# Column-tiled matmuls of a four-layer attention kernel: two tiles of 64 columns instead of four of 32, and a matmul of 33 columns that gives a unit's numerator and denominator

## The chip, the cores and the metric

The kernel runs on one core of one Trainium2 chip. The metric is the device time of one execution in microseconds (us), lower is better. TensorE is called PE here, VectorE DVE, ScalarE ACT, GpSimd POOL and SyncE SP, as in the profile.

## The reference, cut to what matters

Four residual layers follow each other on x (2048 rows of 1024, bf16): A, B, A, B. Each normalizes the rows, projects to q, k and v in 32 heads of 32 columns, mixes, and projects back. A is a linear attention, with a feature map made of two softmaxes. B is softmax attention:

```python
scores = jnp.einsum("bhqd,bhkd->bhqk", q, k) * (Dh ** -0.5)
p = _softmax(scores, axis=-1)
o = jnp.einsum("bhqk,bhkd->bhqd", p, v)
return (lambda x, *d: x.transpose(*d))(o, 0, 2, 1, 3).reshape(B, S, D) @ wo

x = x + _A_ref(_layernorm(x, axis=-1), A_wqkv, A_w_phi, A_wo)
x = x + _B_ref(_layernorm(x, axis=-1), B_wqkv, B_wo)
x = x + _A_ref(_layernorm(x, axis=-1), A_wqkv, A_w_phi, A_wo)
x = x + _B_ref(_layernorm(x, axis=-1), B_wqkv, B_wo)
```

## The kernel before, in words

The program is a list of operations (engine, duration, what it waits for, buffers, priority) and a planner, `Sched.run`, that lays them out when the kernel is built. The planner keeps a clock of its own for each engine, takes the ready operation of the lowest priority number whose buffers can be had, and so writes a fixed order of instructions for each engine. On the chip an engine works through its own order and waits on semaphores. Durations and latencies (`LAT`, `act_us`, `dve_us`, `MM`, `SWITCH`) only shape this order, and some sixty constants (`KL`, `P0`, `MOST`, `LOAD` and the like) set due times and limits. A pair of an A and a B layer is one turn of `for layer in range(2)`: layer 0 and layer 1 below mean these pairs.

**Attention.** The queries are four chunks of 512 (`qc`), the heads eight groups of four (`g`). A turn is one (qc, g): 2 x 8 x 4 = 64 units, each 128 keys by 512 queries of one head, so 32 turns and 2048 units in each layer. For a unit the kernel makes scores on PE (L1191; a contraction of 32, so up to four units stand on different row tiles of the array and run together), the exponential, and the product with V (L1386). The functions:

- `group` takes up to three units from the front, has PE write their scores into one half (three banks) of six PSUM banks, and ACT takes the exponential of all of them in one instruction (L1251, 1536 wide). The two halves alternate.
- With a "third", it takes only two units for ACT (1024 wide), and the third bank goes to a unit some 25 ahead, which DVE makes into an exponential. It does so only if at least `MIX` groups lie between, if DVE's queue is below `THIRD_LOAD`, and if bank 7 is taken. `attach` adds a fourth unit in bank 7 where that is free and DVE's queue allows (`BOTH_LOAD`, `LOAD`). `MOST` limits the DVE units of a turn; it is 0 in the first turn of each layer.
- DVE's exponential is a conversion out of PSUM (`convert`, L1339) for each unit, and then for a batch of `NB` = 2 units `exp_dve`: two masks (L1153) and two tensor_tensor (L1158).
- The product with V: for two units four matmuls of 32 columns each, tile positions 0, 32, 64 and 96: V of one head and a block of ones, for each unit. So numerators stand in 64 rows of the accumulator bank 6, and the denominators, 32 times over, in the other 64; for the other pair of heads (`pp` = 1) the halves change places. `T` is the copy out of PSUM (L1402). Denominators go through 2 KB transfers (L1436), a reciprocal (L1441), a scratch tensor and a broadcast back (L1442, L1444), one transfer (L1447) brings the second pair's numerators beside the first's, and L1449 multiplies.

**Fillers between.** While attention runs, PE also computes the projections that are due (`mmg2`, which calls `mm`; with bank list `FIL`, that is bank 7 alone, `mm` splits each matmul into four of 32 columns at L584, so that the array stays in column tiling), in layer 0 also the keys of the next A layer (`a_keys` with `alone`, L836). Where the plan finds PE's last 3.4 us less than 75% worked it puts in matmuls of no use (`idle` through L584 with `onesD`, `idle_acc` at L1644 with zero weights). Outside attention, matmuls use the whole array (L580).

A change between row tiles, column tiles and the whole array is a "mode" of the planner ("r", "c", "n"), with `SWITCH` = 0.106 us for each change.

**V.** `b_v` projects V for 128 keys and 512 columns and evacuates it (`evac`, L1053 on ACT or L1054 on DVE) with the columns of each head side by side. **Output.** `b_out` multiplies the `oT` tiles with `B_wo`, loaded by `slab` in four transfers of 256 KB. The last turn of a layer (`end`) has a path of its own without transfers.

Of the kernel before, what the change touches and what calls it, by code (L numbers as in the profile page):

```python
# [11 lines left out]
ALU = mybir.AluOpType  # L12
# [12 lines left out]
class Buf:  # L25


    __slots__ = ("kind", "size", "cls", "banks", "left", "at", "with_", "key")

    def __init__(self, kind, size, cls, banks=None):  # L30
        self.kind, self.size, self.cls, self.banks = kind, size, cls, banks
        self.left, self.at, self.with_ = 0, None, ()

# [12 lines left out]
LAT = {"PE": 0.28, "ACT": 0.07, "DVE": 0.17, "POOL": 0.2, "SP": 2.0, "AQ": 2.0}  # L46
# [13 lines left out]
class Sched:  # L60
    def __init__(self, sbuf_bytes, quota):
# [7 lines left out]
        self.queue = {}  # L69
        self.idle = self.idle_acc = self.wants = self.pace = None  # L70
# [124 lines left out]
    def run(self):  # L195
# [28 lines left out]
        while left:  # L224
            moved = False
            for e in engines:
                if busy[e] > t + 1e-9 or not ready[e] and (e != "PE" or t < WARM_UP):
                    continue
                skipped, held = [], []
# [88 lines left out]
                busy[e] = t + d  # L318
                order.append(pick)
# [56 lines left out]
XQ = 7.72  # L376
# [9 lines left out]
NB = 2  # L386
SPLIT = (lambda i: False, lambda i: False)
LAG = 8
KL = (17, 32)
KS = (3.31, 6.5)  # L390
VS = (5, 6.75)
# [7 lines left out]
KD = 9.84  # L399
HALF = (False, True)  # L400
VH = 3.5
V_LATE = (None, ((8.47, 5.81), (77.66, 6.67)))
Q_LATE = (lambda c, g: 105 + 6 * g if c == 2 else 10.43 + 22.43 * g, lambda c, g: 120 + 12 * g)
QL = (11, 11.19)
AW = 26
OUT_AT = (232, 260.02, 273.59)
GO = 2.54
BO = 290.14
PT = 3.13
QB = 18.16  # L410
PH = (1, 22, 43)
LA = 1.59
AHEAD_AT = 4
P0 = (131.15, 178.4, 234.98)
GAPS = (1.5, 1.5, 3.19)
PK = (142, 184, 261.5)
STEP = 2.4
AWAY = (-10, 12)
MIX = (lambda i: (2, 2, 1, 2)[i // 8], lambda i: (0, 0, 0, 0)[i // 8])
LOAD = (2.03, 2.38)  # L420
AHEAD = (24, 25)
SLACK = 12
THIRD_LOAD = (3.79, 1.29)
BOTH_LOAD = (0.74, 0.56)
EARLY = (80, 80)
BEHIND = -4
NEAR = (8, 8)
LEAD = 0.14
MOST = (lambda i: 0 if i < 1 else 15, lambda i: 0 if i < 1 else 26)
# [10 lines left out]
MM = 0.2165  # L440
WARM = 60
WIRE = 360.0
BACKLOG = 1.0
KV_MM = 0.042
# [3 lines left out]
def kernel(  # L448
# [26 lines left out]
    B_o = B_wo.rearrange("(po pi) f -> pi po f", pi=P)  # L475
# [13 lines left out]
    zero = const.tile([P, DH], BF16, tag="zero")  # L489
# [19 lines left out]
    work = const.tile([P, 2, NB * C512], BF16, tag="work")  # L509
# [51 lines left out]
    def fixed(cls, spots):  # L561
        b = Buf("ps", 0, cls, spots)
        return b, lambda: work[:, b.at[0] - 8, :].rearrange("p (a b) -> p a b", b=C512)

# [12 lines left out]
    def mm(out_, lhsT, rhs, start, stop, cols):  # L577
# [4 lines left out]
        for k in range(4):  # L582
            ks = slice(32 * k, 32 * k + 32)
            nc.tensor.matmul(out_[ks, :], lhsT=lhsT[:, ks], rhs=rhs, start=start, stop=stop,  # L584
                             tile_position=(0, 32 * k), skip_group_check=True)

    MM4 = 0.2165
# [577 lines left out]
    def attention(base, kT, vT, q_of, gate, most, mix, turns, pos, ahead, near, load, split_at, early, third_load, both_load):  # L1165
# [166 lines left out]
        def convert(so, u, s_b, s_v, turn):  # L1332
# [10 lines left out]
            if k == NB - 1:  # L1343
                close(pair)
# [335 lines left out]
```

## Time and profile before

| what | us |
|---|---|
| median of 3 runs (2149.93 to 2153.79) | 2151.93 |
| the profiled execution | 2151.16 |
| its span, first to last instruction | 2149.0 |
| stretch 0 to 324, layer 0's linear attention and projections | 324 |
| stretch 324 to 1176, layer 0's softmax attention | 852 |
| stretch 1176 to 1376, layer 1's linear attention and projections | 200 |
| stretch 1376 to 2136, layer 1's softmax attention | 760 |

In the views, "busy" of an engine is the union of its instructions' times; a matmul is shown some 0.38 us long although the next starts 0.22 us later, since matmuls are pipelined, and an ACT or DVE instruction also overlaps the next a little. So a mean duration is longer than the step from one start to the next, and steps are read from the timeline. In a line of the grouped views stand line, engine, operation, output and input, shapes, count, then busy us and the mean ns of one, then idle time before them. "128*32" is a matmul on 128 rows and 32 columns of the array.

### The profile page before, as it was taken

How to read it: one execution, taken by the hardware profiler on the slowest of the kernel's cores; microseconds unless marked ns; L12 is line 12 of the kernel's file. 1: busy time of each engine (PE TensorE's matmuls, PEld its weight loads, DVE VectorE, ACT ScalarE, POOL GpSimd, SP SyncE). 2: the span in 40 equal slices, each digit the busy share in tenths (PEclk: the TensorE clock that was granted, in tenths of full speed). 3: DMA queues.
4: the chain of work that ended last, by engine and by line, in shares of the span. 5: the costliest groups of instructions: out<-in, count | busy, mean ns of one | idle time of the engine just before them, and what ended most of it. 6: DMA issues, size and time to landing. Idle time of an engine off the chain costs nothing. (4 is left out here: it accounts for less than half of the span.)

```text
span 2149.0 us, 64468 instructions
## 1 busy us (share of the span) xinstructions
PE 2104.6 (98%) x27498; PEld 784.6 (37%) x27498; DVE 1742.8 (81%) x3163; ACT 1934.9 (90%) x2050; POOL 27.4 (1%) x78
## 2 busy tenths in 40 slices
PE   9999999999999999999999999999999999999999
PEld 5543443333333333333333434533333333333333
DVE  8866552666567889997887876289999999999998
ACT  7337669999999999999999576899999999999998
POOL 1000000000000000000000000000000000000000
PEclk9999999999999999999999999999999999999999
DMA  7730231112233433342454312211111222121111
GB/s 232 162 71 14 75 78 26 33 45 54 59 94 94 120 101 110 93 139 58 128 156 138 110 40 69 62 30 35 39 47 43 52 52 55 38 71 54 49 44 36
DMA packets 258392, 161.53 MB, mean 75 GB/s; under 512 B 150712, under 2 KB 232632, under 8 KB 258104
## 3 DMA queue, kind: packets, MB, share of 16 engines
q1 hardware_dynamic: 258104, 157.41, 27.4%
q8 instruction: 215, 3.52, 0.7%
q14 instruction: 73, 0.60, 0.1%
HBM read 90.51 MB, written 29.87 MB: 56 GB/s over the span
## 5 line engine op out<-in xcount | busy, mean ns | idle before, releaser
L1251 ACT ACTIVATE arena<-psum 128x1536 bf16<-128x1536 f32 (+1 forms) x1349 | 1578.4, 1370 | 6.7 <-PE psum L1191 5.1
L584 PE MATMUL psum<-arena 128*32 128x512 bf16 (+1 forms) x9536 | 632.3, 365 | 7.0 <-DVE arena L814 1.7
L1386 PE MATMUL psum<-arena 128*32 128x512 bf16 x4096 | 608.2, 383 | 4.1 <-DVE arena L1402 3.0
L1386 PE MATMUL psum<-arena,ones_bf 128*32 128x512 bf16 x4096 | 608.0, 383 | 0.5 <-issue 0.5
L1191 PE MATMUL psum<-arena 32*128 32x512 bf16 x4096 | 530.7, 384 | 18.4 <-ACT arena L1251 15.5
L1339 DVE TENSOR_SCALAR arena<-psum 128x512 uint16<-128x512 f32 x618 | 417.8, 682 | 91.6 <-PE psum L1191 86.2
L580 PE MATMUL psum<-arena 128*128 128x512 bf16 (+1 forms) x1968 | 435.1, 372 | 2.2 <-DVE arena L848 0.7
L1158 DVE TENSOR_TENSOR arena<-arena,work 128x1024 bf16<-128x1024 bf16 x618 | 424.1, 686 | 13.3
L1191 PEld LDWEIGHTS <-arena 32*128 32x128 bf16 x4096 | 146.7, 91 | 553.3 <-issue 549.6
L584 PEld LDWEIGHTS <-arena 128*32 128x32 bf16 x9536 | 210.5, 95 | 257.2 <-issue 158.1
L580 PEld LDWEIGHTS <-arena 128*128 128x128 bf16 x1968 | 185.7, 98 | 217.7 <-issue 19.4
L1386 PEld LDWEIGHTS <-arena 128*32 128x32 bf16 x4096 | 165.3, 95 | 212.7 <-issue 150.1
L1153 DVE TENSOR_SCALAR work<-arena 128x1024 uint16<-128x1024 uint16 x618 | 239.3, 417 | 2.4
L1386 PEld LDWEIGHTS <-ones_bf 128*32 128x32 bf16 x4096 | 163.8, 95 | 25.1 <-issue 9.0
L1054 DVE CAST arena<-psum 128x512 bf16<-128x512 f32 (+1 forms) x120 | 69.3, 577 | 60.8 <-PE psum L584 47.5
L801 ACT ACTIVATE arena<-psum 128x512 bf16<-128x512 f32 x80 | 43.5, 594 | 71.7 <-PE psum L580 57.4
L1402 DVE COPY arena<-psum 128x512 f32<-128x512 f32 x126 | 85.8, 681 | 12.4 <-PE psum L1386 11.6
L805 DVE TENSOR_REDUCE arena<-arena 128x32 f32<-128x1024 bf16 x64 | 77.6, 1213 | 16.2 <-ACT arena L801 15.9
L953 ACT ACTIVATE arena<-psum 128x512 bf16<-128x512 f32 x112 | 61.9, 597 | 31.6 <-PE psum L580 28.7
L626 ACT ACTIVATE arena<-xR 128x1024 bf16<-128x1024 bf16 x40 | 42.3, 1057 | 44.9 <-DVE xR L1028 39.0
L814 DVE TENSOR_TENSOR arena<-psum,arena 128x1024 bf16<-128x1024 f32 x64 | 77.6, 1212 | 4.0 <-DVE arena L808 0.4
L1028 DVE TENSOR_TENSOR xR<-xR,psum 128x512 bf16<-128x512 bf16 x64 | 42.6, 682 | 15.1 <-PE psum L580 15.0
(98 smaller groups left out, 1008.4 us busy)
## 6 DMA issues: line engine op xcount, KB each, us to landing
arena<-in_B_wqkv_dram SPq DMA_DIRECT2D x69, 256.0 KB
arena<-rd SPq DMA_DIRECT2D x62, 256.0 KB
xa<-arena SPq DMA_DIRECT2D x48, 256.0 KB
arena<-in_A_wqkv_dram SPq DMA_DIRECT2D x40, 256.0 KB
arena<-in_B_wo_dram SPq DMA_DIRECT2D x40, 256.0 KB
arena<-arena SPq DMA_DIRECT2D x256, 32.0 KB
arena<-wd_k SPq DMA_DIRECT2D x32, 256.0 KB
arena<-arena SPq DMA_DIRECT2D x62, 128.0 KB
```

The source lines that it names most:

```text
L580: nc.tensor.matmul(out_, lhsT=lhsT, rhs=rhs, start=start, stop=stop, skip_group_check=True)
L584: nc.tensor.matmul(out_[ks, :], lhsT=lhsT[:, ks], rhs=rhs, start=start, stop=stop, tile_position=(0, 32 * k), skip_group_check=True)
L805: red = op("DVE", dve_us(1024), lambda ev=ev, sv=sv: nc.vector.reduce_sum(out=sv(), in_=ev().rearrange("p s (h d) -> p (s h) d", d=DH), ax ...
L814: ml = op("DVE", dve_us(1024), lambda vpv=vpv, wv_=wv_, sv=sv: nc.vector.tensor_tensor(out=wv_()[:, :, :, 0:DH], in0=vpv().rearrange("p (h ...
L1054: return soon(op("DVE", dve_us(n), lambda: nc.vector.tensor_copy(out=dst(), in_=src()), [dep], bufs, prio))
L1153: return sch.later("DVE", n * C512 / 3840 + 0.065, lambda: nc.vector.tensor_scalar(out=out_().bitcast(U16), in0=y_v().bitcast(U16), scalar ...
L1158: return sch.later("DVE", n * C512 / 1920 + 0.065, lambda: nc.vector.tensor_tensor(out=y_v(), in0=y_v(), in1=in1(), op=what), [dep], [e_b, ...
L1191: nc.tensor.matmul(out=out_, lhsT=kT[g][1]()[r, pp, d * P:(d + 1) * P], rhs=q_of[(qc, g)][1]()[r, (pp + j // 2) % 2, :], start=True, stop= ...
L1251: ex = make("ACT", act_us(w * C512), lambda: nc.scalar.activation(out=e_v()[:, 0:w * C512], in_=s_v()[:, 0:w * C512], func=ACT.Exp, scale= ...
L1339: pair["got"].append(sch.later("DVE", dve_us(512) + 0.01, lambda: nc.vector.tensor_scalar(out=e_v().bitcast(U16)[:, k, :], in0=s_v(), scal ...
L1386: nc.tensor.matmul(out=a_v()[col:col + 32, :], lhsT=v_v()[:, kc % 4, o:o + DH] if what == 0 else ones_bf[:], rhs=ev()[:, x * C512:(x + 1) ...
L1402: cp = op("DVE", dve_us(512), lambda t_v=t_v, a_v=a_v: nc.vector.tensor_copy(out=t_v(), in_=a_v()), [last], [a_b, t_b], prio - 4)
```

## The change

- `mm` makes two matmuls of 64 columns (tile positions 0 and 64) where it made four of 32; so does `idle_acc`.
- V is kept with its heads interleaved: column d * 16 + h, and 16 columns of ones behind, set by POOL once per tile (32 x 16 + 16 = 528 columns a row). The weights of a head, with a step of 16 elements, are then 33 columns, the last of them ones. One matmul of 33 columns at position 0 or 64 gives numerator and denominator of a unit; two units take two matmuls instead of four. The last turn keeps the old form.
- What keeps 32 columns (L836, the 32-column sums of the A layer, the last turn) is a mode of its own, "b".
- Numerators now stand in rows 0 to 31 and 64 to 95, denominators in rows 32 and 96. One transfer (L1447) becomes two, and the rows of `B_wo` are loaded in the matching order (`wo_slab`; the tail's own copy of the last rows comes in five transfers, in both layers).
- DVE's exponential works on batches of `NB` = (2, 3) units by layer; its order is now mask, multiply, mask, add, with one scratch tile. The unused "split" form goes.
- The planner has other latencies and durations, another 40 or so constants, and a rule (`HOLD`): while a score group is ready but has no banks, PE doesn't begin another matmul if that would make the score, and with it ACT, late.

The diff, cut to its core:

```diff
-LAT = {"PE": 0.28, "ACT": 0.07, "DVE": 0.17, "POOL": 0.2, "SP": 2.0, "AQ": 2.0}
+LAT = {"PE": 0.285, "ACT": 0.2, "DVE": 0.13, "POOL": 0.2, "SP": 2.0, "AQ": 2.0}
...
+                if e == "PE" and self.live.get("S", 0) and any(
+                        i[0] == 0 and i[3].bufs and i[3].bufs[0].cls == "S" and i[3].bufs[0].at is None for i in ready[e]):
+                    free = min((b.until for b in self.slots if b.parts == 0 and b.until > t), default=None)
+                    if free is not None and free > t:
+                        then = busy["ACT"] + sum(i[3].dur for i in ready["ACT"] if i[3].bufs and i[3].bufs[0].cls == "S")
+                        reach = lambda at: max(0.0, at + SWITCH + MM + LAT["PE"] - then)
+                        if reach(max(free, t + MM)) - reach(free) > HOLD * (free - t):
+                            continue
...
-NB = 2
-SPLIT = (lambda i: False, lambda i: False)
+NB = (2, 3)
...
-LOAD = (2.03, 2.38)
-AHEAD = (24, 25)
-SLACK = 12
-THIRD_LOAD = (3.79, 1.29)
-BOTH_LOAD = (0.74, 0.56)
+LOAD = (2.24, 2.19)
+AHEAD = (25, 32)
+SLACK = 12.87
+THIRD_LOAD = (6.08, 1.29)
+BOTH_LOAD = (1.05, 0.11)
...
-MOST = (lambda i: 0 if i < 1 else 15, lambda i: 0 if i < 1 else 26)
+MOST = (lambda i: 0 if i < 1 else 12, lambda i: 16 if i < 1 else 29)
...
-        for k in range(4):
-            ks = slice(32 * k, 32 * k + 32)
+        for k in range(2):
+            ks = slice(64 * k, 64 * k + 64)
             nc.tensor.matmul(out_[ks, :], lhsT=lhsT[:, ks], rhs=rhs, start=start, stop=stop,
-                             tile_position=(0, 32 * k), skip_group_check=True)
+                             tile_position=(0, 64 * k), skip_group_check=True)
...
+        if "ones" not in done:
+            done["ones"] = op("POOL", 0.3, lambda: nc.gpsimd.memset(v_v()[:, :, C512:C512 + 16], 1.0), [m], [v_b], prio)
+        e = evac(eng, lambda: v_v()[:, t, 0:C512].rearrange("p (d h) -> p h d", h=16)[:, 8 * halves[0]:8 * halves[-1] + 8, :],
+                 lambda: pv()[:, 0:n].rearrange("p (h d) -> p h d", d=DH), m, [pb, v_b], prio, n)
...
+        m = mask(x_v, 0x007F, 0x3F00, pair["got"])
+        z = both(x_v, ALU.mult, m)
+        p = mask(y_v, 0x7F80, EXP2_D, [z])
+        return both(y_v, ALU.add, p)
...
+                                for k in range(2):
+                                    ev, x = e_of[us[k]]
+                                    w = v_v()[:, kc % 4, :].rearrange("p (d h) -> p h d", h=16)[:, 4 * (g % 4) + 2 * pp + k, :]
+                                    ex = ev()[:, x * C512:(x + 1) * C512]
+                                    if not end:
+                                        nc.tensor.matmul(
+                                            out=a_v()[64 * k:64 * k + DH + 1, :], lhsT=w, rhs=ex,
+                                            start=(d == 0 and u == 0), stop=(d == 7 and u == 1),
+                                            tile_position=(0, 64 * k), skip_group_check=True)
+                                        continue
...
+                mv = [dma(prio, lambda T=T, k=k: nc.sync.dma_start(
+                    out=T[0][1]()[64 * k + 32:64 * k + 64, :], in_=T[1][1]()[64 * k:64 * k + 32, :]),
+                    [rc, T[1][2]], [T[0][0], T[1][0]], kb=64) for k in range(2)]
```

196 lines of the change are left out of this document (94 added, 102 removed).

## The prediction

> **What bounds the kernel now.** I read the page first, then the table by stages, then the groups by form within each attention, and last the timeline, for steps.
>
> ```profile
> span 2149.0 us, 64468 instructions
> PE 2104.6 (98%) x27498; PEld 784.6 (37%) x27498; DVE 1742.8 (81%) x3163; ACT 1934.9 (90%) x2050; POOL 27.4 (1%) x78
> ```
>
> ```profile
> core 0: us, PE busy (x) PEld busy (x) DVE busy (x) ACT busy (x) POOL busy (x), PEclk, DMA share, GB/s
> 324.00:1176.00 852.00, 833.52 (x12267) 282.12 (x12265) 651.14 (x1135) 840.65 (x738) 10.39 (x25) 1.00 0.33 89
> 1376.00:2136.00 760.00, 746.32 (x10977) 257.00 (x10975) 723.97 (x1377) 757.81 (x673) 0.00 (x0) 1.00 0.17 45
> ```
>
> PE looks like the bound, but the second table shows ACT idle for 852.00 - 840.65 = 11.4 us in layer 0's attention and 760.00 - 757.81 = 2.2 us in layer 1's, where PE has 18.5 and 13.7. DVE has 201 us idle in layer 0 and 36 in layer 1. The two attentions are 1612 of 2149 us, and ACT ends last in both. PE's share must also be read with what it does for nothing:
>
> ```profile
> L584 PE MATMUL psum<-xR,onesD 128*32 128x512 bf16 x512 | 41.2, 382 | 0.8 <-DVE arena L1066 0.6
> L1644 PE MATMUL psum<-xR,zero 128*32 128x512 bf16 x228 | 18.8, 381 | 0.0
> ```
>
> These two rows of the whole span are the matmuls of no use, 41.2 + 18.8 = 60 us of PE that can go without loss. So PE has some 90 us of room in the attentions and ACT 13.6.
>
> What ACT does, layer 0's rows first, then layer 1's:
>
> ```profile
> L1251 ACT ACTIVATE arena<-psum 128x1536 bf16<-128x1536 f32 x443 | 643.3, 1548 | 4.1 <-PE psum L1191 2.9 <-PE psum L1386 1.0
> L1251 ACT ACTIVATE arena<-psum 128x1024 bf16<-128x1024 f32 x235 | 264.1, 1124 | 0.4 <-PE psum L1191 0.4
> L1339 DVE TENSOR_SCALAR arena<-psum 128x512 uint16<-128x512 f32 x248 | 169.3, 684 | 87.8 <-PE psum L1191 83.2 <-PE psum L836 1.9 <-PE psum L1386 0.8
> 324.00:1176.00 852.00, 815.11 (x678) 1.00 0.33 89
> ```
>
> ```profile
> L1251 ACT ACTIVATE arena<-psum 128x1536 bf16<-128x1536 f32 x337 | 481.1, 1552 | 0.9 <-PE psum L1191 0.6
> L1251 ACT ACTIVATE arena<-psum 128x1024 bf16<-128x1024 f32 x331 | 333.3, 1125 | 1.3 <-PE psum L1191 1.2
> L1339 DVE TENSOR_SCALAR arena<-psum 128x512 uint16<-128x512 f32 x370 | 248.5, 680 | 3.8 <-PE psum L1191 3.1
> L1153 DVE TENSOR_SCALAR work<-arena 128x1024 uint16<-128x1024 uint16 x370 | 143.3, 415 | 0.0
> 1376.00:2136.00 760.00, 757.01 (x668) 1.00 0.17 45
> ```
>
> The last row of each fence is the union of L1251 in that stretch. Layer 0: 443 x 3 + 235 x 2 = 1799 units on ACT, 815.11 / 1799 = 0.453 us a unit, and 248 on DVE. Layer 1: 337 x 3 + 331 x 2 = 1673 units, 757.01 / 1673 = 0.4525, and 370 on DVE. The two rows as equations (443a + 235b = 815.11, 337a + 331b = 757.01) give a step of 1.36 us for three units and 0.90 for two. So the attention time falls by 0.45 us for each unit that moves to DVE, and otherwise only by ACT's idle time. That is the measure for every part below.
>
> **The change part by part.**
>
> *Two tiles for four.* PE's steps:
>
> ```profile
> 1500.14 0.39 PE L1191 MATMUL psum<-arena 32*128 32x512 bf16 x3
> 1500.46 0.39 PE L1386 MATMUL psum<-arena 128*32 128x512 bf16 x1
> ...
> 1500.68 0.38 PE L1386 MATMUL psum<-arena 128*32 128x512 bf16 x1
> ...
> 1500.90 0.38 PE L1386 MATMUL psum<-arena 128*32 128x512 bf16 x1
> ...
> 1501.12 0.38 PE L1386 MATMUL psum<-arena 128*32 128x512 bf16 x1
> ...
> 1501.44 0.39 PE L1191 MATMUL psum<-arena 32*128 32x512 bf16 x3
> ```
>
> ```profile
> 322.41 1.46 PE L580 MATMUL psum<-arena 128*128 128x512 bf16 x6
> 323.80 0.39 PE L1191 MATMUL psum<-arena 32*128 32x512 bf16 x3
> ```
>
> Four tiles of 32 columns are replaced every 0.22 us (1500.68, 1500.90, 1501.12). Two of 64 cover the same 128 columns, so I take the same step; nothing is saved in the stream, and the product with V stays at one step for two units although half of each 64 is empty. What can change is the edge. Score to column tiles takes 0.32 (1500.14 to 1500.46), column tiles to score 0.32 (1501.12 to 1501.44), while from the whole array (last of six starts at 322.41 + 5 x 0.216 = 323.49) it takes 0.31. Leaving one tile is 0.01 cheaper than leaving four; leaving two I put between, 0 to 0.01 each for 678 + 668 = 1346 score groups: 0 to 13 us of PE. On the other side, the first column step after a score is 1500.68 - 1500.46 = 0.22, with at most 0.01 for loading 32 columns that nothing covers; 64 columns might show twice that, up to 0.01 x 1346 = 13 us more, and 33 almost none. Both ends lie within PE's 60 us of useless work, so the value I take for the time is 0; without that cover it is -13 to +13. [...]
>
> The mode "b" adds changes around L836 (in layer 0's attention six bursts; 12 changes of 0.1 us if kept together, 96 if torn apart: 1 to 10 us of PE, in the same cover, 0 taken).
>
> *Batches of three in layer 1.*
>
> ```profile
> 1501.77 1.42 DVE L1158 TENSOR_TENSOR arena<-arena,work 128x1024 bf16<-128x1024 bf16 x2
> ...
> 1503.71 0.75 DVE L1153 TENSOR_SCALAR work<-arena 128x1024 uint16<-128x1024 uint16 x2
> ...
> 1504.38 0.68 DVE L1339 TENSOR_SCALAR arena<-psum 128x512 uint16<-128x512 f32 x1
> ...
> 1504.98 0.68 DVE L1054 CAST arena<-psum 128x512 bf16<-128x512 f32 x1
> ```
>
> A conversion's step is 0.60 (1504.38 to 1504.98), a mask's 0.75 - 0.415 = 0.335 (two masks, less the last one's 415 ns); two tensor_tensor, the second needing the first, 1.42 - 0.69 = 0.73. The code's own form, n/3840 + 0.065 for a mask, gives 0.332 and fits; for a tensor_tensor, n/1920 + 0.065, it gives 0.60, which leaves 0.13 for needing the one before. A batch has four such instructions, so 0.26 us fixed: 0.13 a unit in twos, 0.087 in threes, -0.043. The new order has three links of need instead of two, 0.13 each: per unit the same (3/3 for 2/2). 370 units x 0.043 = 16 us of DVE; a unit costs DVE 0.60 + (2 x 0.335 + 2 x 0.60 + 0.17)/2 = 1.62, so 10 units more, x 0.4525 = **-5 us**. Ends: 0 if time goes by elements alone; if half of a mask's step is fixed in all four, 0.64 a batch, 0.107 a unit, 40 us, 24 units, -11.
>
> *The first turn of layer 1* may now have 16 DVE units (15 in threes); before it had none:
>
> ```profile
> 1376.00:1405.00 29.00, 28.43 (x437) 12.46 (x436) 4.73 (x8) 29.00 (x27) 0.00 (x0) 1.00 0.09 21
> 1405.00:2096.00 691.00, 679.13 (x9999) 231.58 (x9996) 680.16 (x1298) 688.83 (x615) 0.00 (x0) 1.00 0.18 47
> ```
>
> DVE (third figure) works 4.73 of the first 29.00 us and 680.16 of the next 691. The free 24 us hold 15 units of 1.6. 15 x 0.4525 = 6.8; **-6 us** taken, since a unit 32 ahead needs its queries landed. Ends 0 and -7. In layer 0 nothing of the kind: its first turn stays at 0.
>
> *Layer 0's limits.* 235 of 678 groups have a third, 35%, about what `MIX` lets through (one in three, in eight turns one in two), and 248 - 235 = 13 had a fourth. A higher `THIRD_LOAD` frees little; 0 taken. The end: DVE's 201 idle us would hold 124 units, -56 us.
>
> *New latencies and the hold rule.*
>
> ```profile
> PE psum L1191 <- ACT arena L1251: 15.5, 50, 1.0
> ```
>
> Scores wait visibly for ACT's release 50 times; an order that has PE free at the release can win back ACT's idle 13.6 us at best. I take half, **-6 us**; an order that serves it worse could lose as much.
>
> *V and its evacuation.* Interleaved writes are in no row. The V casts of layer 1's attention:
>
> ```profile
> L1054 DVE CAST arena<-psum 128x256 bf16<-128x256 f32 x48 | 20.0, 416 | 6.2 <-PE psum L584 6.1
> L1054 DVE CAST arena<-psum 128x512 bf16<-128x512 f32 x28 | 19.1, 682 | 15.7 <-ACT arena L1251 13.0 <-PE psum L584 2.6
> ```
>
> The evacuation reads 32-bit PSUM at 1 ns an element; I take no change, 0. If a scattered write doubled it: 39 us of DVE, 24 units, +11; a gain I exclude, the same elements are read. The 16 ones blocks run on POOL, idle at 99%. SP has 62 more transfers in the attentions:
>
> ```profile
> 704.08 0.51 SPq L1447 DMA_DIRECT2D arena<-arena  x1
> ```
>
> 62 x 0.51 = 32 us over 1612; behind them stand the next turn's denominators, wanted only when the output projection comes tens of us later. 0; cover gone only in the last turns, where +2 at most.
>
> *Sum:* 2151.2 (profiled; the median is 2151.9) - 5 - 6 - 6 = **2134 us**.
>
> **The rivals.**
>
> 1. *DVE takes much more in layer 0.* If the looser limits fill half of its 201 idle us: 62 units x 0.453 = -28, 2106. For: the idle time. Against: `MIX` binds.
> 2. *Conversions come late behind longer instructions: slower.* In layer 1 ACT's step for two units is 0.90. To be ready, a score needs 0.39 (its duration at 1500.14), so DVE must have read its third 0.90 + 0.90 - 0.39 = 1.41 after both began; less its own 0.68, it may stand behind an instruction of 0.73. A tensor_tensor of two units (0.60 to 0.73) just fits. One of three (1536/1920 + 0.065 = 0.865, with need 0.99) is late by 0.14 to 0.26. At 0.14 for all 331 groups with a third +46, for half +23; the terms -5 and -6 stay, the -6 of waiting turns to +6: 2151 + 23 - 11 + 6 = 2169. It decides from 0.73 on, if the plan lets conversions fall behind such an instruction.
> 3. *PE takes over.* If the 64-column loads and torn "b" bursts cost their 13 + 10 and the useless matmuls don't make room, the gains of 17 are eaten: 2151 to 2157. [...]
> 4. *The pair doesn't stream together.*
>
> ```profile
> L584 PE MATMUL psum<-arena 128*32 128x512 bf16 (+1 forms) x9536 | 632.3, 365 | 7.0 <-DVE arena L814 1.7
> L1386 PE MATMUL psum<-arena 128*32 128x512 bf16 x4096 | 608.2, 383 | 4.1 <-DVE arena L1402 3.0
> L1386 PE MATMUL psum<-arena,ones_bf 128*32 128x512 bf16 x4096 | 608.0, 383 | 0.5 <-issue 0.5
> ```
>
> Then each of the (9536 + 4096 + 4096) / 4 = 4432 column steps costs 0.22 more: 3130. The trace has tiles of 32 side by side; I see no reason for 64 to differ.
>
> **How the numbers follow.** Forecast 0.62 (own range 2115 to 2150), rival 1 0.13, rival 2 0.17, rival 3 0.06, rival 4 0.02. Range 2100 to 2171: rival 1's middle and rival 2's, the unknown V write (+11) within. About 0.2% (4 us) is what a measurement here tells from no change. Faster: 0.13 + 0.57 of the forecast = 0.70; same: 0.03 of the forecast and 0.04 of rival 3 = 0.07; slower: 0.02 of the forecast, 0.17, 0.02 of rival 3 and 0.02 = 0.23.
>
> **What would show it.** In the profile after: column steps still 0.22; score edges 0.31 to 0.33; L1339 in layer 1 at some 395 (370 + 10 + 15), with 15 of them fed in the first turn, and near 248 in layer 0; L1251's union shorter by 11 us in layer 1; ACT's idle halved. The forecast is wrong if ACT's idle before L1251 grows in layer 1 with L1339 as releaser of L1191 (rival 2), if layer 0's L1339 rises past 290 (rival 1), or if useless matmuls vanish while PE steps grow (rival 3).

## The result, and the profile after

The changed kernel takes 2266.26 us (median of 4 runs, 2265.07 to 2269.2), the kernel before 2151.16 (4 runs, 2149.93 to 2153.79). The ratio is 1.0535 with a 95% interval of 1.0517 to 1.0554: some 115 us slower, where 2134 (2100 to 2171) was forecast. The profiled execution took 2269.2 us, with a span of 2267.4.

The diff moves lines: scores are L1211 now (L1191 before), ACT's exponential L1269 (L1251), V's product L1398 (L1386), the fills and matmuls of no use through `mm` L599 (L584), conversions L1356 (L1339), the evacuations L1072 on ACT and L1073 on DVE (L1053, L1054).

The page of the changed kernel, and then its table by stages. The columns of the table are the length of the stretch, then the busy time of PE, weight loads, DVE, ACT and POOL, then the granted clock:

```profile
span 2267.4 us, 46159 instructions
PE 2165.5 (96%) x18374; PEld 885.0 (39%) x18374; DVE 1830.6 (81%) x2972; ACT 1987.3 (88%) x2049; POOL 29.4 (1%) x94
```

```profile
330.00:1230.00 900.00, 854.67 (x7600) 330.27 (x7600) 682.67 (x1127) 860.99 (x741) 10.21 (x26) 0.99 0.31 81
1435.00:2254.00 819.00, 778.38 (x6544) 306.95 (x6543) 779.56 (x1192) 773.63 (x677) 0.15 (x1) 0.99 0.17 42
```

The attentions took 852 and 760 us in the table before, whose last stretch begins at 1376, 3 us behind layer 1's first score at 1372.6; they take 900 and 819 now: some 104 of the 115 us lie there. ACT was idle for 11.4 and 2.2 us in them; now for 900.00 - 860.99 = 39 and 819.00 - 773.63 = 45. PE's idle time rose as well, from 18.5 and 13.7 to 45 and 41. DVE's rose from 201 and 36 to 217 and 39. All three large engines have more room than before: each waits for another.

The groups by form in layer 1's attention show that the number of units on DVE came out as forecast:

```profile
L1269 ACT ACTIVATE arena<-psum 128x1536 bf16<-128x1536 f32 x317 | 445.1, 1464 | 25.6 <-PE psum L1211 20.9 <-PE psum L1398 2.4 <-ACT arena L1269 0.4
L1269 ACT ACTIVATE arena<-psum 128x1024 bf16<-128x1024 f32 x351 | 346.2, 1037 | 17.1 <-PE psum L1211 14.3 <-DVE arena L1466 0.3
L1356 DVE TENSOR_SCALAR arena<-psum 128x512 uint16<-128x512 f32 x393 | 266.1, 691 | 22.1 <-PE psum L1211 20.7 <-ACT arena L1269 1.3
```

393 units are on DVE (395 forecast, 370 before). Only, ACT now stands idle ahead of its exponentials for 25.6 + 17.1 us, and what ends most of that wait is PE's score (L1211). Who makes the scores late is in the list of waits of the whole span (us in total, times, longest):

```profile
ACT arena L1269 <- PE psum L1211: 62.3, 105, 4.1
PE psum L599 <- DVE arena L1073: 37.8, 49, 2.0
PE psum L1211 <- DVE arena L1356: 2.6, 8, 0.7
```

The same two waits before:

```profile
ACT arena L1251 <- PE psum L1191: 5.1, 11, 1.1
PE psum L584 <- DVE arena L1054: 0.3, 1, 0.3
```

The fills on PE wait for DVE's casts out of bank 7 (L1073 casts V and K): 0.3 us before, 37.8 now. The casts, by form, over the whole span; first before, then after:

```profile
L1054 DVE CAST arena<-psum 128x512 bf16<-128x512 f32 x72 | 49.3, 685 | 54.6 <-PE psum L584 41.4 <-ACT arena L1251 13.0
L1054 DVE CAST arena<-psum 128x256 bf16<-128x256 f32 x48 | 20.0, 416 | 6.2 <-PE psum L584 6.1
L1053 ACT CAST arena<-psum 128x512 bf16<-128x512 f32 x24 | 14.0, 582 | 12.7 <-PE psum L580 12.6
L1053 ACT CAST arena<-psum 128x256 bf16<-128x256 f32 x16 | 5.7, 398 | 2.5 <-PE psum L580 1.9 <-DMA arena<-arena 0.5
```

```profile
L1073 DVE CAST arena<-psum 128x512 bf16<-128x512 f32 x72 | 75.6, 1050 | 42.0 <-PE psum L599 41.9
L1073 DVE CAST arena<-psum 128x256 bf16<-128x256 f32 x48 | 59.5, 1240 | 2.1 <-PE psum L599 1.9
L1072 ACT CAST arena<-psum 128x512 bf16<-128x512 f32 x24 | 40.3, 1801 | 2.8 <-PE psum L595 2.8
L1072 ACT CAST arena<-psum 128x256 bf16<-128x256 f32 x16 | 18.3, 1431 | 1.6 <-PE psum L595 1.6
```

V's cast of 256 columns takes 1.24 us on DVE instead of 0.42, and 1.43 on ACT instead of 0.40. In the groups of 512 columns only 16 casts each are V's; the others, of K, write side by side as before. So V's own take 0.685 + (75.6 - 49.3)/16 = 2.33 us on DVE and 0.582 + (40.3 - 14.0)/16 = 2.23 on ACT (from busy times; from the means (24 x 1.801 - 8 x 0.582)/16 = 2.41). In the trace the 16 on DVE last 2.33 us each on average, the 16 on ACT 2.41. What one such cast does is to be seen in the timeline of layer 1's attention (start, us, engine; the rows between are left out):

```profile
1595.70 5.10 ACT L1269 ACTIVATE arena<-psum 128x1536 bf16<-128x1536 f32 x4 [0.23 <-PE psum L1211]
...
1598.92 0.39 PE L1211 MATMUL psum<-arena 32*128 32x512 bf16 x2
1599.13 1.23 DVE L1073 CAST arena<-psum 128x256 bf16<-128x256 f32 x1
...
1599.24 0.44 PE L1398 MATMUL psum<-arena 128*33 128x512 bf16 x2
...
1600.41 0.74 PE L599 MATMUL psum<-arena 128*64 128x256 bf16 x10 [0.73 <-DVE arena L1073]
...
1601.08 0.39 PE L1211 MATMUL psum<-arena 32*128 32x512 bf16 x3
...
1601.52 2.79 ACT L1269 ACTIVATE arena<-psum 128x1536 bf16<-128x1536 f32 x2 [0.72 <-PE psum L1211]
```

The cast runs from 1599.13 to 1600.36. The next fill on PE needs the same bank 7, and PE, which works in order, stands for 0.73 us. The score behind that fill starts at 1601.08, ACT has been done since 1600.80 and stands for 0.72 us. Here the 0.73 us of PE arrive on ACT whole.

### The profile page after: what moved, and what is told of

The parts are those of the page before. It is cut to its first block, busy times and chain, and to the rows that moved or that the text cites. A ratio compares the mean times of both kernels' runs of the same rounds, so it can differ in the third digit from the quotient of the medians.

```text
span 2267.4 us, 46159 instructions
## 1 busy us (share of the span) xinstructions
PE 2165.5 (96%) x18374; PEld 885.0 (39%) x18374; DVE 1830.6 (81%) x2972; ACT 1987.3 (88%) x2049; POOL 29.4 (1%) x94
## 4 chain that ended last, share of the span: by engine, by line
PE 54%; DVE 29%; ACT 8%; issue 5%; DMA 3%; SPq 1%; DVEq 0%; ACTq 0%
PE psum L599 15%; PE psum L595 13%; PE psum L1398 11%; PE psum L1211 10%; DVE arena L1356 7%; ACT arena L1269 4%; DVE arena L1073 4%; DVE work L1178 3%; DVE arena L1178 3%; ACT arena L1072 2%; DVE work L1173 2%; DVE arena L1173 2%; DVE arena L1419 1%; DVE arena L824 1%; DMA arena<-in_A_wqkv_dram 1%
## 5 line engine op out<-in xcount | busy, mean ns | idle before, releaser
L1269 ACT ACTIVATE arena<-psum 128x1536 bf16<-128x1536 f32 (+1 forms) x1348 | 1594.5, 1287 | 80.3 <-PE psum L1211 62.3
L599 PE MATMUL psum<-arena 128*64 128x512 bf16 (+1 forms) x4768 | 646.1, 372 | 53.9 <-DVE arena L1073 36.9
L1398 PE MATMUL psum<-arena 128*33 128x512 bf16 x3968 | 618.7, 397 | 4.5 <-DVE arena L1419 3.2
L1211 PE MATMUL psum<-arena 32*128 32x512 bf16 x4096 | 546.7, 386 | 17.9 <-ACT arena L1269 11.0
L1356 DVE TENSOR_SCALAR arena<-psum 128x512 uint16<-128x512 f32 x639 | 435.4, 691 | 109.2 <-PE psum L1211 106.7
L599 PEld LDWEIGHTS <-arena 128*64 128x64 bf16 x4768 | 234.4, 109 | 316.1 <-issue 235.8
L1211 PEld LDWEIGHTS <-arena 32*128 32x128 bf16 x4096 | 135.4, 91 | 516.1 <-issue 512.4
L1398 PEld LDWEIGHTS <-arena 128*33 128x33 bf16 x3968 | 249.1, 144 | 210.9 <-issue 152.0
L1178 DVE TENSOR_TENSOR work<-arena,work 128x1536 bf16<-128x1536 bf16 (+2 forms) x256 | 211.0, 824 | 6.3
L1178 DVE TENSOR_TENSOR arena<-arena,work 128x1536 bf16<-128x1536 bf16 (+2 forms) x256 | 210.5, 822 | 5.5
L1073 DVE CAST arena<-psum 128x512 bf16<-128x512 f32 (+1 forms) x120 | 135.1, 1126 | 44.1 <-PE psum L599 43.8
L1173 DVE TENSOR_SCALAR arena<-arena 128x1536 uint16<-128x1536 uint16 (+2 forms) x256 | 126.5, 494 | 4.6
L1173 DVE TENSOR_SCALAR work<-arena 128x1536 uint16<-128x1536 uint16 (+2 forms) x256 | 125.5, 490 | 4.4
L824 DVE TENSOR_REDUCE arena<-arena 128x32 f32<-128x1024 bf16 x64 | 77.7, 1214 | 15.0 <-ACT arena L820 14.3
L1072 ACT CAST arena<-psum 128x512 bf16<-128x512 f32 (+1 forms) x40 | 58.6, 1653 | 4.4 <-PE psum L595 4.4
```

The costliest lines, as they stand in the source:

```text
L824: red = op("DVE", dve_us(1024) + 0.107, lambda ev=ev, sv=sv: nc.vector.reduce_sum(out=sv(), in_=ev().rearrange("p s (h d) -> p (s h) d", d ...
L1072: return op("ACT", act_us(n), lambda: nc.scalar.copy(out=dst(), in_=src()), [dep], bufs, prio)
L1073: return soon(op("DVE", dve_us(n), lambda: nc.vector.tensor_copy(out=dst(), in_=src()), [dep], bufs, prio))
L1173: return sch.later("DVE", n * C512 / 3840 + 0.065, lambda: nc.vector.tensor_scalar(out=out_().bitcast(U16), in0=y_v().bitcast(U16), scalar ...
L1178: return sch.later("DVE", n * C512 / 1920 + 0.065, lambda: nc.vector.tensor_tensor(out=out_(), in0=y_v(), in1=x_v(), op=what), [dep], [e_b ...
L1211: nc.tensor.matmul(out=out_, lhsT=kT[g][1]()[r, pp, d * P:(d + 1) * P], rhs=q_of[(qc, g)][1]()[r, (pp + j // 2) % 2, :], start=True, stop= ...
```

## The experiments

The theory: V's **scattered write** is the cause, through bank 7 and PE, as in the timeline. Its rivals: the weights with a **step** of 16 load slowly; **two tiles** of 64 columns, or the single matmul of 33, cost PE time; the **new order** of the instructions (constants, latencies, batches of three, hold rule) is worse. Medians below are to be set against the kernel before on the same chips, 2147.8 to 2150.4 us, above which the changed kernel's 2266.3 lies by some 117 (115 against its own pair of runs).

**V head by head, 33 columns side by side** (`contig`): everything of the change, with its order on PE, DVE and ACT, but V written and read without a step.

```diff
...
-        e = evac(eng, lambda: v_v()[:, t, 0:C512].rearrange("p (d h) -> p h d", h=16)[:, 8 * halves[0]:8 * halves[-1] + 8, :],
+        e = evac(eng, lambda: v_v()[:, t, :].rearrange("p (h x) -> p h x", x=33)[:, 8 * halves[0]:8 * halves[-1] + 8, 0:DH],
...
-                                    w = v_v()[:, kc % 4, :].rearrange("p (d h) -> p h d", h=16)[:, 4 * (g % 4) + 2 * pp + k, :]
+                                    w = v_v()[:, kc % 4, :].rearrange("p (h x) -> p h x", x=33)[:, 4 * (g % 4) + 2 * pp + k, :]
```

> The changed kernel with V kept head by head (33 columns side by side, the last of them ones) instead of interleaved; all else, the plan's order included, as in the changed kernel. Theory L (the interleaved layout is the cause: V casts at 1.2 to 2.4 us instead of 0.4 to 0.7, and 33 weights at a step of 16 elements that show 0.05 us after each score group): 2135 to 2165 us, V casts back at 0.42 and 0.69 us, the step after a score back from 0.27 to at most 0.24. Theory P (new order, hold rule and batches of three are the cause): 2230 to 2266. Theory T (64-column tiles are the cause): 2230 to 2266.

Measured: 2181.55 us, ratio 1.0151 [1.0134, 1.0168], between the theories: above L's 2165, far below the 2230 of P and T. Some 85 of the change's 117 us go with the layout (83 of 115 by the ratios, each to its own chip), 32 remain. DVE's casts are back at 0.42 us, and both waits are much shorter:

```profile
L1073 DVE CAST arena<-psum 128x256 bf16<-128x256 f32 x48 | 20.1, 420 | 1.9 <-PE psum L599 1.9
ACT arena L1269 <- PE psum L1211: 18.6, 35, 3.3
PE psum L599 <- DVE arena L1073: 5.4, 15, 0.9
```

Since the order of instructions is the same, the two attentions can be compared piece by piece. First the stretches of this kernel, then the union of the exponentials (L1269) over both attentions, here and in the changed kernel:

```profile
326.00:1190.00 864.00, 834.99 (x7595) 287.31 (x7594) 656.86 (x1127) 845.79 (x739) 10.38 (x26) 1.00 0.31 85
1393.00:2170.00 777.00, 754.28 (x6543) 261.58 (x6541) 743.67 (x1192) 758.58 (x675) 0.38 (x1) 1.00 0.17 44
```

```profile
sum 1641.00, ACT 1576.35; mean ACT 788.18
sum 1719.00, ACT 1592.47; mean ACT 796.23
```

The attentions are 1719 us long in the changed kernel and 1641 here, 78 less (the step of the weights, priced next, is a small part of it). ACT's idle time makes 48 of the 78 (84.4 us there, 36.6 here). V's casts on ACT itself make 14 (L1072 takes 12.07 and 7.87 us there, 3.53 and 2.13 here). The remaining 16 are the same exponentials, which overlap one another less there: by their means they add up to 762 x 1.474 + 585 x 1.044 = 1734 us there and 762 x 1.510 + 585 x 1.076 = 1780 here, for unions of 1592 and 1576. So the scattered write reaches ACT in two ways, through PE's waits and through ACT's own casts. The waits of the fills for DVE's casts grow by 37.8 - 5.4 = 32 us, about half of what these casts got longer by.

**The step of the weights alone** (`contig_read16`): the same order again, V written side by side, weights read with a step of 16. The heads' columns are mixed up by it, and POOL first fills the other half of each row with ones (32 more fills, 9.6 us on POOL).

```diff
...
-                                    w = v_v()[:, kc % 4, :].rearrange("p (h x) -> p h x", x=33)[:, 4 * (g % 4) + 2 * pp + k, :]
+                                    w = v_v()[:, kc % 4, :].rearrange("p (d h) -> p h d", h=16)[:, 4 * (g % 4) + 2 * pp + k, :]
```

> The head by head kernel (2181.6) in the same order, V written side by side, but the 33 weights read at a step of 16 elements (columns mixed up; the other half of a row is filled with ones on POOL first). It isolates the price of the weight load that the changed kernel has. Theory L by the steps: the step after a score that begins with a V matmul goes from 0.228 back to 0.27, about 590 times 0.044 = 26 us of PE, of which 10 to 30 show: 2190 to 2212. If the write alone matters: 2179 to 2186.

Measured: 2187.4 us, ratio 1.0182 [1.0167, 1.0197], just above the range for the write alone (2179 to 2186). So the step of the weights costs 6 us, and the scattered write, at the same order, 2266.3 - 2187.4 = 79 us (76 by the ratios). The 6 us are visible in PE's timeline; first the contiguous kernel, then this one:

```profile
1559.88 0.39 PE L1211 MATMUL psum<-arena 32*128 32x512 bf16 x3
1560.20 0.61 PE L1398 MATMUL psum<-arena 128*33 128x512 bf16 x4
1560.74 0.39 PE L1211 MATMUL psum<-arena 32*128 32x512 bf16 x3
```

```profile
1561.51 0.39 PE L1211 MATMUL psum<-arena 32*128 32x512 bf16 x3
1561.83 0.65 PE L1398 MATMUL psum<-arena 128*33 128x512 bf16 x4
1562.42 0.39 PE L1211 MATMUL psum<-arena 32*128 32x512 bf16 x3
```

From a score to the first column matmul 0.32 in both; from there over two steps to the next score 0.54 and 0.59 us. It is the first load of 33 weights with a step that shows 0.05 us: in the traces the first column step behind a score takes 0.228 us in the contiguous kernel and 0.272 in this one (medians of 469), behind a fill 0.216 in both (129). Some 20 us of PE come to 6 us of time.

**The write alone, in the kernel before** (`write8`), and **the read alone** (`read8`), each with a step of 8 elements within a half tile, so that the heads are mixed up:

```diff
-        e = evac(eng, lambda: v_v()[:, t, hs], lambda: pv()[:, 0:n], m, [pb, v_b], prio, n)
+        e = evac(eng, lambda: v_v()[:, t, hs].rearrange("p (a d h) -> p a h d", a=len(halves), h=8),
+                 lambda: pv()[:, 0:n].rearrange("p (a h d) -> p a h d", a=len(halves), d=DH), m, [pb, v_b], prio, n)
...
-                                                lhsT=v_v()[:, kc % 4, o:o + DH] if what == 0 else ones_bf[:],
+                                                lhsT=v_v()[:, kc % 4, 256 * (g % 4 // 2):256 * (g % 4 // 2) + 256].rearrange("p (d h) -> p h d", h=8)[:, 4 * (g % 2) + j, :] if what == 0 else ones_bf[:],
```

> The kernel before, with V written interleaved within each half of 256 columns (a step of 8 elements) and read side by side, so that heads are mixed up: this isolates the scattered write. Theory L: the casts of 512 take over 1.2 us on DVE and ACT, those of 256 over 0.8; the time goes to 2180 to 2230. Theories P and T: 2150 to 2156.

> The kernel before, with V written side by side and its weights read at a step of 8 elements (heads mixed up, 32 columns still): this isolates the scattered weight load. Theory L: the step after a score rises from 0.227 by 0.03 to 0.05, which is 15 to 35 us of PE; ACT lets 10 to 30 of it show: 2160 to 2185. Theories P and T: 2150 to 2156.

Measured: the write 2224.78 us, 1.0356 [1.0341, 1.0372]; the read 2159.28, 1.0049 [1.0034, 1.0064], 10 us, between its two ranges. The write alone, with no other edit and the same order of instructions, costs the kernel before 75 us, and its profile has the same marks:

```profile
L1054 DVE CAST arena<-psum 128x256 bf16<-128x256 f32 x48 | 62.5, 1302 | 5.1 <-PE psum L584 5.1
ACT arena L1252 <- PE psum L1192: 36.8, 74, 1.5
PE psum L584 <- DVE arena L1054: 29.4, 43, 1.6
```

So the scattered write is shown to cost 75 to 79 us twice, in two kernels with different orders.

**Two tiles of 64 and one matmul of 33** in the kernel before, at its own order on ACT and DVE (`before_two`).

```diff
-        for k in range(4):
-            ks = slice(32 * k, 32 * k + 32)
+        for k in range(2):
+            ks = slice(64 * k, 64 * k + 64)
...
+                                    if not end:
+                                        nc.tensor.matmul(
+                                            out=a_v()[64 * k:64 * k + DH + 1, :], lhsT=ones33[:], rhs=ex,
...
```

> The kernel before in its own order of instructions, but with two tiles of 64 columns and one matmul of 33 columns for each unit. The 33 weights are a constant tile of ones, so V isn't read (every attention output is 1); the rows of B_wo aren't reordered; the second transfer of the pair is there. It asks what the tiles alone do. Theory T: what the head by head layout left of the loss (32 us) comes from the tiles: 2170 to 2190. Theory P: the 32 us come from the new order and constants, and the tiles do nothing: 2143 to 2156.

Measured: 2151.38 us, 1.0012 [1.0002, 1.0021]. The kernel's 33 weights are a constant tile, so that V isn't read; with that limit, what names the change moves the time by 3 us, and as a cause of the loss it falls.

**The planner told the truth** (`after_truth`): the changed kernel, with V's casts planned at 2.2 and 1.1 us on DVE, 2.25 and 1.3 on ACT.

```diff
...
-                 lambda: pv()[:, 0:n].rearrange("p (h d) -> p h d", d=DH), m, [pb, v_b], prio, n)
+                 lambda: pv()[:, 0:n].rearrange("p (h d) -> p h d", d=DH), m, [pb, v_b], prio, n, {("DVE", 512): 2.2, ("DVE", 256): 1.1, ("ACT", 512): 2.25, ("ACT", 256): 1.3}[eng, n])
```

> The changed kernel with its interleaved V, whose planner is told what the scattered V casts take on the chip (2.2 and 1.1 us on DVE, 2.25 and 1.3 on ACT instead of 0.60, 0.34, 0.48 and 0.27). If the casts cost because the plan lays matmuls behind them too early: 2200 to 2235. If the held bank and the engines' time cost whatever the plan: 2250 to 2275.

Measured: 2239.95 us, 1.0416 [1.0400, 1.0432]: 26 us better, between the two ranges expected. Wrong durations in the plan are a part of the loss; the order that the planner finds with the right ones leaves most of it. The layers differ: from first to last score, layer 1's attention takes 788 us (818 in the changed kernel, 777 in the contiguous one), layer 0's 906 (899 and 864), where ACT stands once for 14.3 and once for 6.6 us for a score while PE works off fills. The fills' wait for casts falls to 11.7 us over the whole span (37.8 in the changed kernel), so that this order loses mostly by other waits.

The other kernels ask where the 32 us between the contiguous kernel and the kernel before come from. **All old constants, latencies and twos in the contiguous kernel**, and no hold rule (`contig_oldplan`):

```diff
-LAT = {"PE": 0.285, "ACT": 0.2, "DVE": 0.13, "POOL": 0.2, "SP": 2.0, "AQ": 2.0}
+LAT = {"PE": 0.28, "ACT": 0.07, "DVE": 0.17, "POOL": 0.2, "SP": 2.0, "AQ": 2.0}
...
-NB = (2, 3)
+NB = (2, 2)
...
-THIRD_LOAD = (6.08, 1.29)
-BOTH_LOAD = (1.05, 0.11)
+THIRD_LOAD = (3.79, 1.29)
+BOTH_LOAD = (0.74, 0.56)
...
```

> The same head by head layout, and besides the planner's constants, latencies, durations and batches of two of the kernel before, without the hold rule: what is left of the change is two tiles of 64 columns, the matmul of 33 columns and the transfers that go with it. Theory L: 2140 to 2165. Theory P: near 2150, and at least 60 us under the run with the new plan in the same layout. Theory T: 2230 or more, as the tiles are still there.

Measured: 2228.81 us, 1.0374 [1.0357, 1.0390], worse still: far above what theories L and P expected, and just under the 2230 of theory T, against which `before_two` speaks. Layer 1's linear part, from the last score of layer 0 to the first of layer 1, takes 240 us here (197 before), and one wait in it stands out:

```profile
ACT arena L973 <- DMA arena<-qf: 26.2, 1, 26.2
```

A load on SP's queue lands late in this order, and this linear part is 43 of the 79 us by which the run is slower than the kernel before. The attentions too are longer than in the kernel before, 858 and 789 us from first to last score for 852 and 763: the old plan doesn't give its time back to the new code.

**Without the hold rule** (`contig_nohold`) and **with twos in layer 1** (`contig_nb2`), both from the contiguous kernel:

```diff
-                if e == "PE" and self.live.get("S", 0) and any(
+                if False and e == "PE" and self.live.get("S", 0) and any(
...
-NB = (2, 3)
+NB = (2, 2)
```

> The head by head kernel without the hold rule; the rest of the plan is made anew by the same constants. If the rule is what costs the 32 us that remain: 2145 to 2165. If the rule helps: 2190 or more. If another order is only another order: within 15 us of 2182.

> The head by head kernel (2181.6) with batches of two in layer 1. Layer 0 is unchanged up to where layer 1 begins. If batches of three make conversions late: 2160 to 2172 and layer 1's attention under 768 us. If threes help by 5: 2183 to 2192. If only the order differs: within 12 of 2182.

Measured: 2183.41 us, 1.0159 [1.0143, 1.0174], the rule moves the time by 2 us; 2200.95, 1.0234 [1.0215, 1.0252], under the new constants twos are 19 us worse than threes, all of it in layer 1's attention (796 us for 777).

**One term at a time in the kernel before**: batches of three in layer 1 with the new order within a batch (`before_nb3`), 16 units in its first turn (`before_first`), the new latencies and DVE durations (`before_newlat`).

```diff
-        m = mask(x_v, 0x007F, 0x3F00, pair["got"], [e_b, x_b])
-        p = mask(p_v, 0x7F80, EXP2_D, [m], [e_b, x_b])
-        z = both(x_v, ALU.mult, p)
-        return z if pair["split"] else both(p_v, ALU.add, z)
+        m = mask(x_v, 0x007F, 0x3F00, pair["got"])
+        z = both(x_v, ALU.mult, m)
+        p = mask(y_v, 0x7F80, EXP2_D, [z])
+        return both(y_v, ALU.add, p)
...
-MOST = (lambda i: 0 if i < 1 else 15, lambda i: 0 if i < 1 else 26)
+MOST = (lambda i: 0 if i < 1 else 15, lambda i: 16 if i < 1 else 26)
...
-LAT = {"PE": 0.28, "ACT": 0.07, "DVE": 0.17, "POOL": 0.2, "SP": 2.0, "AQ": 2.0}
+LAT = {"PE": 0.285, "ACT": 0.2, "DVE": 0.13, "POOL": 0.2, "SP": 2.0, "AQ": 2.0}
...
```

> The kernel before with batches of three in layer 1, and the new order within a batch (mask, multiply, mask, add). The prediction's term: -5, so 2142 to 2147. Theory P, or conversions that come late behind longer instructions: 2155 to 2180, with more waits of ACT for scores than the 5 us before.

> The kernel before with one constant changed: DVE may take 16 units in the first turn of layer 1 (before: none). The prediction's term: -6, so 2141 to 2146. Theory P (any new order loses what the old constants were fitted to): the units move but the time is 2150 to 2175.

> The kernel before with nothing but the new latencies (LAT) and the five corrected DVE durations in the planner: same instructions, another order. If such an order by itself is worth some per cent (Theory P): 2165 to 2200. If order hardly matters: 2145 to 2158.

Measured: 2169.9 us, 1.0091 [1.0069, 1.0113]; 2152.47, 1.0013 [1.0003, 1.0022]; 2174.53, 1.0121 [1.0106, 1.0136]. None of the three gains. Units on DVE did rise, to 636, 630 and 637 of 4096 (618 before), and the time did not fall. The places differ: of the 20 us of batches of three 13 lie in layer 1's linear part (210 us for 197), where ACT stands once for 11.0 us for a load, and 5 in the attentions; the 26 us of the latencies and durations lie in the attentions.

**Is any other order worse?** A planner's number is changed by 0.2 to 1%, which changes no operation: `SWITCH` from 0.106 to 0.107 (`before_switch`, `contig_switch`), `MM` from 0.2165 to 0.217 or 0.216 (`before_mm`, `contig_mm`).

```diff
-SWITCH = 0.106
+SWITCH = 0.107
...
-MM = 0.2165
+MM = 0.217
```

> The kernel before, with one number of the planner, the cost of a mode change, set from 0.106 to 0.107 us. Nothing else is changed: the same operations and the same limits, but the planner's clock drifts and it lays out another order. Theory S (any other order, laid out with constants that were found for one order, loses some tens of us): 10 to 40 us slower than the kernel before, some 2160 to 2190. Theory E (the 32 us that are left between the contiguous kernel and the kernel before come from its edits, and the layout of the order alone matters little): within 5 us of 2149.

> The kernel before, with the planner's duration of a matmul set from 0.2165 to 0.217 us, a change without meaning that gives another order. Theory S: 10 to 40 us slower than the kernel before. Theory E: within 5 us of it. Two such runs also show how far two orders of one and the same program lie apart.

> The contiguous kernel (2181.6 us) with the planner's cost of a mode change set from 0.106 to 0.107 us. Theory S: the contiguous kernel's own order is one of many, not better than others for it, so that this lies anywhere from 2160 to 2215. Theory E: within 5 us of 2182, since the edits are the same.

> The contiguous kernel with the planner's duration of a matmul set from 0.2165 to 0.216 us. Theory S: anywhere from 2160 to 2215. Theory E: within 5 us of 2182.

Measured: 2155.7 us, 1.0024 [1.0014, 1.0033]; 2149.23, 0.9991 [0.9982, 1.0001]; 2179.77, 1.0131 [1.0116, 1.0147]; 2186.32, 1.0161 [1.0144, 1.0178]. These orders of one program lie within 7 us of each other. That any other order loses tens of us falls, and so it is unlikely that the 32 us are the chance of an order. It isn't excluded: a load that landed late in one order, that of `contig_oldplan`, had ACT wait for 26.2 us.

**The latencies, once more**: the new latencies and four durations out of the contiguous kernel (`contig_oldlat`), and ACT's alone, 0.2 for 0.07, into the kernel before (`before_actlat`).

```diff
-LAT = {"PE": 0.285, "ACT": 0.2, "DVE": 0.13, "POOL": 0.2, "SP": 2.0, "AQ": 2.0}
+LAT = {"PE": 0.28, "ACT": 0.07, "DVE": 0.17, "POOL": 0.2, "SP": 2.0, "AQ": 2.0}
...
-LAT = {"PE": 0.28, "ACT": 0.07, "DVE": 0.17, "POOL": 0.2, "SP": 2.0, "AQ": 2.0}
+LAT = {"PE": 0.28, "ACT": 0.2, "DVE": 0.17, "POOL": 0.2, "SP": 2.0, "AQ": 2.0}
```

> The contiguous kernel with the old latencies and the four old durations, everything else new. Theory L2 (the latencies and durations are most of the 32 us that the contiguous kernel loses to the kernel before): 2150 to 2165 us. Theory E (the 32 us come from the edits or the other constants): 2175 to 2190. If it is slower still, the new constants were found for the new latencies and don't fit the old ones, and the parts can't be told apart in this way.

> The kernel before with one of the new latencies alone: the planner's latency of ACT is 0.2 instead of 0.07 us, so that it counts a released score bank 0.13 us later. Theory L (the new ACT latency makes the planner put the next score later than PE could begin it, and ACT waits): as slow as with all the new latencies and durations, 2165 to 2180 us. Theory D (it is another of them, the DVE latency or one of the four durations): within 5 us of the kernel before, as the orders that differ by a number without meaning were.

Measured: 2168.77 us, 1.0094 [1.0078, 1.0110], and 2181.44, 1.0151 [1.0134, 1.0169]. The first lies 21 us above the kernel before of its own chip, where the contiguous kernel lay 32 above: the latencies and durations are 11 of the 32, between the two theories. The second is 34 us slower than the kernel before, more than theory L expects, and not for its reason: the attentions, from first to last score, are 4 and 5 us longer, and the rest is layer 1's linear part with the wait met already:

```profile
ACT arena L953 <- DMA arena<-qf: 22.1, 1, 22.1
```

So the 117 us are, as far as the runs tell: scattered write 76 to 79, step of the weights 6, new latencies and durations 11, two tiles some 3, and about 18 that stay open. For those 18 batches of three, the other constants and the smaller edits of the code (the mode "b", the order within a batch, the loads of `B_wo` by rows) remain, and no run tells them apart: threes cost 20 in the kernel before and save 19 under the new constants, and the latencies cost 26 there and 11 here, so that the effects don't add up. No version was clearly faster than the kernel before.

## Why the prediction was wrong, point by point

- **V and its evacuation** is the step that failed: "I take no change, 0". It rested on a row of casts that write side by side, read as if the reading of 32-bit PSUM set their pace, and so as if the target's layout couldn't matter. The scattered cast takes three to four times as long (1.24 us for 0.42 at 256 columns on DVE). The reading of the rows was wrong twice more: the 28 casts of 512 columns taken for V's are K's, and stay at 682 ns after the change; and V's casts on ACT, the engine that ends last, weren't counted, although they grew by (40.3 - 14.0) + (18.3 - 5.7) = 39 us, 14 of them in the attentions.
- **The price put on the doubt** failed with it: "39 us of DVE, 24 units, +11". The casts in the attentions grew by (75.6 - 49.3) + (59.5 - 20.0) = 66 us on DVE, and ACT's there by 14; the attentions lost 78 us by the layout (1719 for 1641). By the prediction's measure 66 us are 41 units, 18 us, and in layer 0, where DVE has 200 us to spare, nothing. But the cast holds the one bank of the fills, PE stands before it in order, and ACT behind PE: in the timeline above a cast of 1.23 us, where 0.42 was usual before, left PE standing for 0.73 us and ACT for 0.72, and in layer 0, where DVE has room, the fills waited 17.5 us for casts (L599 <- L1073, 14 times). Half of the 66 us is seen as waits of the fills. That the attentions' loss lies near the casts' whole growth of 66 + 14 = 80 us isn't shown to be more than chance, since ACT's idle time, its casts and its exponentials each make a part of it.
- **Batches of three -5, first turn -6, latencies -6.** The counts were right (393 DVE units in layer 1, 246 in layer 0, for some 395 and near 248), the gains weren't there. Each alone gave +20, +3 and +26. "Attention time falls by 0.45 us for each unit that moves to DVE" holds only while PE's scores come in time, and L1269's union in layer 1, forecast 11 us shorter, is longer: 765.51 / 1653 = 0.463 us a unit, for 0.4525. After the change ACT's idle time grew by 70 us in the attentions, and the units gained were worth 10.
- **Even without the write** the contiguous kernel, at 2181.6, is above the range. The range counted a worse order at +6, and the new latencies and durations alone made it +26 in the kernel before. So the forecast would have failed without the write too, by less.
- **Two tiles for four, 0 (-13 to +13)**: right, as far as a kernel that doesn't read V tells. The score groups stand 0.32 us from the next column step (1597.51 to 1597.83 in the rows below), and the kernel before with two tiles moved by 3 us.

```profile
1597.51 0.39 PE L1211 MATMUL psum<-arena 32*128 32x512 bf16 x3
1597.83 0.30 PE L599 MATMUL psum<-arena 128*64 128x256 bf16 x2
```

- **Rival 2** (conversions late) doesn't hold: scores wait for conversions only 2.6 us (the last row of the waits after). **Rival 3** (PE takes over, with the matmuls of no use gone) doesn't either; they are still there:

```profile
L599 PE MATMUL psum<-xR,onesD 128*64 128x512 bf16 x218 | 34.1, 385 | 6.6 <-DVE arena L1356 3.4 <-DVE arena L816 1.1 <-DVE arena L1073 0.9
L1663 PE MATMUL psum<-xR,zero 128*64 128x512 bf16 x108 | 17.4, 381 | 0.0
```

They are 52 us (60 before). The prediction took them as room on PE that covers other losses. They don't cover a wait, since the planner puts them where it believes PE free, not where PE comes to stand.
- **Rival 4** (the pair doesn't stream together): no; ten fills of 256 elements in a row take 0.67 us to the next score (1600.41 to 1601.08). That is five pairs of 0.11 us, half a step of 0.22, and 0.1 at the edge (0.32 less 0.22); one after another they would take 1.1.

## What to carry to other kernels

Before taking an evacuation's time as unchanged, look at the layout that it writes, not only at what it reads; the change that is named in a title may be worth nothing and the layout that it needs some 77 us. Price a longer instruction by who waits for the buffer that it holds, on each engine that runs it: where one bank serves an in-order engine, as bank 7 serves PE here, a longer cast can arrive at the bound (0.73 us of PE as 0.72 on ACT in layer 1), and room on the cast's own engine was no cover here: in layer 0's attention DVE was idle for 217 of 900 us, and PE's fills still waited 17.5 us for its casts. And counts that come out as forecast (units moved, steps kept) show that the plan was understood, not that the time follows.

## What the runs showed of the hardware

- A cast out of PSUM to 16-bit columns with a step of 32 bytes took (2.33 - 1.24) / 256 = 4.3 ns a column more on DVE, where side by side it was (0.685 - 0.416) / 256 = 1.05; with a step of 16 bytes (`write8`) it was as slow, 1.30 us for 256 columns. ACT slowed down as DVE did (1.43 for 0.40 us). No run has a smaller step, and none shows the reason.
- 33 weights with a step of 16 elements showed 0.05 us behind a score (0.272 us for 0.228), and nothing behind a fill (0.216 in both).
- In a stretch of layer 0 in which the fills wait for DVE's casts (7.2 of its 100 us), PE's granted clock was 0.97; in the contiguous kernel it was 1.00 there. The means of the two whole executions are 0.992 and 0.998; what of the loss goes with that, no run separates. The columns are length, PE's busy time and the clock; first after, then contiguous:

```profile
350.00:450.00 100.00, 92.53 (x728) 0.97 0.11 27
```

```profile
350.00:450.00 100.00, 99.22 (x822) 1.00 0.14 33
```
